# Loads of the first pair in halves on two queues, column maxima by four maxima instead of a reduce, and a head in another order

## The chip, the cores and the metric

The kernel runs on one core of a Trainium2 chip. The metric is the device time of one execution in microseconds. The engines of the core are named as in the profile: PE (matrix products and transposes), DVE (VectorE), ACT (ScalarE), POOL (GpSimd) and SP, which here only issues transfers.

## The reference, cut to what matters

```
q_s = exp(q - max(q, axis=-1));  q_s /= sum(q_s, axis=-1) + 1e-9
k_s = exp(k - max(k, axis=2));   k_s /= sum(k_s, axis=2) + 1e-9     # over the sequence
kv  = einsum('bhsd,bhse->bhde', k_s, v)
att = einsum('bhsd,bhde->bhse', q_s, kv)          # q, k, v: (8, 8, 576, 64)
x   = att.transpose(0, 2, 1, 3).reshape(4608, 512)
out = maximum(x @ w_in, 0)**2 @ w_out             # 512 -> 2048 -> 512
```

The maximum of q is taken along a row of 64; that of k along the sequence, for each head and column.

## The kernel before

A block is one batch entry of 576 rows, handled as four pairs of heads; block 0 and block 1 prepare their attention with the steps named below, later blocks with other code that the change leaves alone. Each tile `kt`, `qt`, `vt` holds one pair as 128 partitions x 2 heads x 5 records x 64: partition p of the lower half holds five neighbouring rows of the sequence (320 rows), one of the upper half four (256 rows), the fifth being a padding. So the column maximum of k is taken in two steps: along the five records of a partition, then across partitions by a transpose.

The steps of block b and pair p carry the two digits behind their names. `Lk`, `Lq`, `Lv` load. `kmax` (DVE) reduces `kt` to `m`, 128x128; `T` (PE) transposes it; `mc` (DVE) takes the maximum of each row; `spread` (PE) puts it back along the columns; `ke` (DVE) subtracts it from k, one operand being the PSUM bank of `spread`; `kexp` (ACT) is the exponential; `kv` (PE) multiplies with v and with ones; `rs`, `rr` (DVE) make the reciprocal sums and `kvn` (ACT or DVE) scales. On the side of q: `qm` (DVE) the row maximum, `qsub` (POOL) subtracts it from `qt` into `qn`, `qexp` (ACT), `qs` (DVE) sums, `qadd` (POOL), `rc` (DVE) the reciprocal `qs`, `qmul` (POOL) `qn<-qn,qs`, then `qt4`, `qt1` (PE) turn it, `cp`, `cps` (ACT) copy it out, `at` (PE) multiplies with kvn, `xhi` (ACT) and `xlo` (DVE) split the result into two parts for the FFN, and `atl`, `left`, `XL` keep the last 64 rows.

A weight chunk of 512 KB goes through `L` (SP; `raw_i` for w_in, `raw_o` for w_out), `low` and `t` (ACT), `s1` and `s2` (DVE: `bank<-bank,raw` and `w<-raw,bank`), `hi` (ACT: `wi<-w` or `wo<-w`) and `lo` (POOL: `wi<-w,wi`). The FFN of block 0 is `h` (PE: products `x_hi,wi` and `x_lo,wi`), `relu` (ACT), `rm` (DVE), `ghi` (ACT), `glo` (POOL) and `o` (PE). `Z` are products of zeros that keep PE running; 28 of them, the beats, stand at the start. `warm` is one small exponential on ACT.

Every engine works through its instructions in the order in which the program names them: the wrapper `InOrder` chains each to the one before on its engine. That order is a table of tokens, `ORDER`, for the start and for blocks 0 and 1 with the FFN of block 0; a second table, `LIST`, gives all the rest. SP issues its transfers in that order too. Since every call passes through the wrapper, nearly all instructions show its line, L290 before and L292 after; they are told apart by their tiles.

In the instruction lists below, kt_78, kt_79, kt_99 and kt_102 are k of the pairs 0 to 3 of block 0; block 1 uses kt_78 and kt_79 in turn.

Of the kernel before, what the change touches and what calls it, by code (L numbers as in the profile page):

```python
# [50 lines left out]
ORDER = """
Lk00 Lq00 Lk00b warm qm00 qsub00 Lq01 qexp00 qm01 kmax00 qs00 Lk01 Li0 kmax01 T01:0 qsub01 qexp01 qadd00 rc00 Lk02
Lq02 qs01 qadd01 Lq03 T00:1 mc00 mc01 Z3:2 spread01 rc01 kmax02 ti0 lowi0 s1i0 Li1 Lv01 ke01 kexp01 Z4:2 T02:2
qmul01 qt101:3 Lk03 qm02 spread00 qt401:4 cps01 mc02 Lv00 qm03 Li2 qmul00 qt400:5 cp00 qt100:6 Z5:0 kv01:0 s2i0 ti1
Lv02 ke00 Lk10 cps00 spread02 qsub03 qexp03 kmax03 lowi1 qsub02 qexp02 Z3:3 T03:3 qs03 rs01 rr01 kexp00 mc03 Lv03
Li3 cp01 Z3:5 kv00:5 Lq10 spread03 kvn01 at01:1 atl01:6 qadd03 rc03 qmul03 qt403:4 lowi2 qs02 qadd02 rs00 rr00 kvn00
ke02 kexp02 rc02 qmul02 hii0 cp03 atl00:0 ke03 kexp03 s1i1 s2i1 ti2 padv00 kmax10 qt103:5 cps03 at00:2 Lo0 hii1 loi1
kv02:3 rs02 rr02 kvn02 xhi00 qt402:4 kv03:5 cp02 at02:3 Li4 T10:4 s1i2 xlo00 xhi01 rs03 rr03 kvn03 h1_0:2 xlo01
xhi02 loi0 mc10 s2i2 at03:1 left00 lowi3 Lo1 qm10 ti3 xlo02 xhi03 lowo0 qt102:5 hii2 Lk11 Lv10 qsub10 s1i3 s2i3 hii3
xlo03 spread10 ke10 loi2 qexp10 Lo2 h0_0:0 h0_1 qs10 cps02 h1_1 h1_2 h1_3 loi3 Li5 h0_2 to0 s1o0 lowo1 h2_0:3 h2_1  # L60
h2_2 relu1 h3_0:1 kexp10 Lk12 qadd10 rc10 qmul10 lowi4 left01 s2o0 to1 rm1 h0_3 ghi1 glo1 h2_3 kmax11 atl03:4 s1o1
s2o1 padv01 Lo3 ti4 s1i4 left03 hio1 atl02:5 qt410:2 kv10:6 cp10 s2i4 loo1 rs10 rr10 T11:4 h3_1 mc11 h3_2 relu0 rm0
kvn10 hii4 lowo2 spread11 ke11 h3_3 to2 at10:2 loi4 h4_0:0 Li12 ghi0 kmax12 qt110:6 hio0 left02 T12:4 mc12 relu3
h4_1 h4_2 h4_3 loo0 kexp11 Lq11 s1o2 spread12 s2o2 late xhi10 xlo10 lowi5 glo0 o0_3:5 o1_3 o0_0:2 o1_0 hio2 ti5 loo2
ke12 o0_2:4 o1_2 relu2 s1i5 Li6 Lo4 s2i5 lowo3 to3 hii5 loi5 qm11 cps10 o0_1:6 o1_1 Lk20 qsub11 rm2 h5_0:3 h5_1 h5_2
h5_3 s1o3 s2o3 XL03 lowi12 lowi6 ghi2 glo2 o2_3 o2_1 o2_2 o2_0 lowo4 rm3 ghi3 glo3 Li7 ti6 XL00 lowi7 hio3 loo3 o3_3
o3_0 o3_1 o3_2 relu4 Lv12 qexp11 kmax20 kexp12 Lq12 XL01 relu5 XL02 s1i6 s2i6 hii6 loi6 h6_0:1 h6_1 h6_2 h6_3 Lk13
rm4 qs11 qadd11 to4 s1o4 s2o4 Lo5 ghi4 hio4 glo4 loo4 o4_3 o4_2 o4_0 o4_1 atl10:0 Li8 qm12 qsub12 ti7 rm5 ghi5
kv12:3 glo5 lowo5 s1i7 s2i7 hii7 loi7 kmax13 relu6 rm6 h7_0:1 to5 s1o5 lowi8 s2o5 qexp12 qs12 qadd12 h7_1 h7_2 h7_3
rc11 qmul11 left10 T13:0 hio5 ti8 s1i8 Lo6 lowo6 rs12 rr12 kvn12 s2i8 to6 s1o6 qt411:3 Li9 loo5 o5_0 Lv11 o5_1 relu7  # L70
rm7 s2o6 hii8 loi8 o5_3 kv11:1 mc13 ghi6 glo6 ti9 cp11 lowi9 Lo7 lowo7 spread13 hio6 loo6 h8_0:3 h8_1 h8_2 Li10 ke20
rs11 rr11 kvn11 s1i9 s2i9 rc12 qmul12 Lo8 lowo8 at11:1 Li13 Lo10 ke13 to7 s1o7 s2o7 hii9 xhi11 lowi10 o6_3 loi9
xlo11 qt111:0 cps11 ti10 s1i10 s2i10 o5_2 ghi7 lowo10 glo7 o6_0 atl11:0 left11 Li15 hio7 loo7 to8 s1o8 s2o8 Lo11
hii10 h8_3 relu8 o6_2 hio8 rm8 h9_0:1 h9_1 h9_2 h9_3 relu9 o6_1 Lk21 o7_3 lowi15 qt412:0 ghi8 Li11 lowi11 kmax21
kexp13 loo8 loi10 o7_0 cp12 ti11 s1i11 s2i11 rm9 qt112:3 cps12 Lo9 o7_1 Lq13 qm13 lowo9 to9 hii11 o7_2 s1o9 glo8
o8_3 Lo13 at12:0 xhi12 h10_0:3 h10_1 h10_2 h10_3 XL11 Lv13 loi11 h11_0:1 h11_1 xlo12 kv13:0 h11_2 ghi9 glo9 Lq20
h11_3 qsub13 lowo11 relu10 Lo14 Li14 s2o9 ti12 hio9 loo9 o9_3 o8_1 o9_1 rm10 atl12:3 qexp13 s1i12 s2i12 to10 s1o10
s2o10 hii12 loi12 relu11 Lo12 Lv20 lowi13 qs13 qadd13 ti13 kexp20 lowi14 Lo15 Lq21 o8_0 o9_0 s1i13 hio10 loo10 rs13
rr13 kvn13 s2i13 rm11 lowo14 Lv21 WA0 WA1 ko0 ko1 to11 o8_2 o9_2 ghi10 ghi11 h12_0:0 h12_1 h12_2 h12_3 rc13 qmul13
s1o11 s2o11 ti14 s1i14 qsub20 Lq22 hio11 lowo12 qt413:1 left12 XL10 glo10 o10_2 o10_3 Lk22 hii13 relu12 qt113:3  # L80
o10_1 lowo13 cps13 atl13:3 left13 XL13 rm12 kv20:0 s2i14 loo11 XL12 loi13 h13_0:3 h13_1 h13_2 h13_3 hii14 qexp20
o10_0 glo11 o11_3 o11_0 o11_2 o11_1 loi14 to12 cp13 h14_0:1 h14_1 h14_2 h14_3 lowo15 ke21 kexp21 s1o12 s2o12 hio12
loo12 ti15 s1i15 s2i15 relu13 rm13 ghi12 glo12 o12_2 o12_3 o12_1 to13 hii15 loi15 s1o13 s2o13 hio13 loo13 qn20 o12_0
h15_0:3 h15_1 h15_2 h15_3 Lv22 WA2 WA3 ko2 ko3 ghi13 relu14 to14 s1o14 s2o14 to15 glo13 o13_3 o13_1 o13_2 hio14
loo14 o13_0 s1o15 s2o15 hio15 rm14 ghi14 glo14 h16_0:1 relu15 rm15 ghi15 glo15 Bw20 Lk23 WA4 ko4 o14_3 qsub21 at13:3
loo15 o15_3 xhi13 xlo13 o14_0 o15_0 B20 rs20 h16_1 rr20 qexp21 ev3 S3 qn21 ev0 S0 ko6 Bw21 h16_2 o14_1 o15_1 ev1
qh20 ql20 kf20 h16_3 relu16 rm16 ghi16 S1 B21 glo16 o14_2 o15_2 ev2 S2 kh20 kl20 Lq23 h17_0:3 h17_1 h17_2 h17_3
""".split()


# [1246 lines left out]
```

## Time and profile before

| | |
|---|---|
| median of three runs (lowest, highest) | 838.47 us (838.05, 840.71) |
| the profiled execution, its own time | 838.89 us |
| its span, first to last instruction | 837.1 us |
| granted clock of PE, mean | 1.000 |
| busy: PE, DVE, ACT, POOL | 99%, 65%, 58%, 34% |
| HBM, over the span | 214 GB/s |

The span is what the trace covers; 1.8 us of the execution lie around it. Busy shares are means over the whole run. The head, some 47 us in which the first products are prepared, is where the engines other than PE are nearly full, and its rows have to be read by themselves.

### The profile page before, as it was taken

The page shows a single profiled execution, that of the slowest core. Times are in us where ns is not written, and L with a number is a line of the kernel's source. Part 1 is how long each engine was busy: PE and PEld are TensorE (multiplying, and loading weights), DVE is VectorE, ACT ScalarE, POOL GpSimd, SP SyncE. Part 2 cuts the span into 40 slices and gives each one's busy share as a digit, 9 for nine tenths or more (in the row PEclk, how much of TensorE's full clock was granted, in tenths as well). Part 3 has the DMA queues.
Part 4 walks back from the last instruction along what each step waited for, and adds up shares of the span by engine and source line. Part 5 has one row for each costly group of instructions (what it writes and reads, how often), then busy time and mean ns, then how long its engine had stood idle before and what let it go on. Part 6 is the DMA issues. An engine that isn't in the chain of part 4 may idle for free.

```text
span 837.1 us, 12969 instructions
## 1 busy us (share of the span) xinstructions
PE 828.8 (99%) x4286; PEld 678.2 (81%) x4286; DVE 540.8 (65%) x1098; ACT 486.7 (58%) x898; POOL 288.2 (34%) x269
## 2 busy tenths in 40 slices
PE   8999999999999999999999999999999999999997
PEld 6778787888888888888888888888888888888886
DVE  7898888878787789957687887653257132222421
ACT  4888866666656656676667455566464144444411
POOL 4578654467667656242322342211004000000000
PEclk9999999999999999999999999999999999999999
...
GB/s 240 270 186 299 279 287 214 327 215 98 211 256 249 227 283 259 277 281 258 234 252 245 283 159 213 271 187 189 172 233 177 98 227 156 163 166 154 186 55 50
DMA packets 156594, 179.65 MB, mean 215 GB/s; under 512 B 51696, under 2 KB 120304, under 8 KB 156528
## 3 DMA queue, kind: packets, MB, share of 16 engines
...
HBM read 133.69 MB, written 45.09 MB: 214 GB/s over the span
## 4 chain that ended last, share of the span: by engine, by line
PE 90%; DVE 4%; DMA 2%; issue 1%; POOL 1%; ACT 1%; SPq 1%; DVEq 0%; POOLq 0%; ACTq 0%
PE bank L290 90%; DVE m L290 1%; DMA raw_o<-in_moe_w_out_dram 1%; DMA qt<-in_q_dram 1%; SPq L290 1%; DMA raw_i<-in_moe_w_in_dram 0%; POOL qs L290 0%; DVE qs L290 0%; DVE g_lo L290 0%; DVE w L290 0%; POOL qn L290 0%; DVE xf L290 0%; DVE bank L290 0%; DVE r L290 0%; DVE qm L290 0%
## 5 line engine op out<-in xcount | busy, mean ns | idle before, releaser
L290 PE MATMUL bank<-wp,g 128*128 128x512 f32 x648 | 160.7, 390 | 0.0
L290 PEld LDWEIGHTS bank<-wp,g 128*128 128x128 f32 x648 | 120.6, 188 | 24.9
L290 PE MATMUL bank<-x_hi,wi 128*128 128x512 f32 x384 | 131.3, 396 | 0.0
L290 PE MATMUL bank<-xh_T,wp 128*128 128x512 f32 x384 | 130.7, 390 | 0.0
L290 PE MATMUL bank<-wo,g_hi 128*128 128x512 f32 x384 | 120.3, 394 | 0.0
L290 PE MATMUL bank<-xh_B,wp 128*128 128x512 f32 x288 | 98.0, 390 | 0.0
L290 POOL TENSOR_TENSOR qs<-qT,qs 64x640 fp32r<-64x640 f32 (+1 forms) x40 | 64.2, 1604 | 94.4 <-ACT qs L290 63.1
L290 DVE TENSOR_TENSOR c<-c,bank 128x512 f32<-128x512 f32 x48 | 32.9, 686 | 86.7 <-ACT c L290 86.4
L290 PEld LDWEIGHTS bank<-xh_T,wp 128*128 128x128 f32 x384 | 72.1, 188 | 16.3 <-ACT bank L290 1.2
L290 PEld LDWEIGHTS bank<-x_hi,wi 128*128 128x128 f32 x384 | 72.2, 188 | 15.9 <-DVE x_lo L290 0.4
L290 ACT ACTIVATE far<-far 128x512 f32<-128x512 f32 x96 | 60.6, 632 | 41.1 <-DVE far L290 39.9
L290 PEld LDWEIGHTS bank<-wo,g_hi 128*128 128x128 f32 x384 | 70.5, 188 | 14.8 <-ACT g_hi L290 0.4
L290 PE MATMUL bank<-wo,g_lo 128*128 128x512 f32 x192 | 75.0, 391 | 0.0
L290 PE MATMUL bank<-x_lo,wi 128*128 128x512 f32 x192 | 74.9, 390 | 0.0
L290 PE MATMUL bank<-xl_T,wp 128*128 128x512 f32 x192 | 74.8, 389 | 0.0
L290 PE MATMUL bank<-wo_back,g 128*128 128x512 f32 x288 | 71.4, 389 | 0.0
L290 DVE TENSOR_TENSOR g<-far,g 128x512 fp32r<-128x512 f32 x48 | 35.7, 781 | 43.5 <-ACT g L290 43.4
L290 DVE TENSOR_TENSOR far<-far,bank 128x512 f32<-128x512 f32 x48 | 32.9, 685 | 47.7 <-PE bank L290 47.5
L290 PEld LDWEIGHTS bank<-xh_B,wp 128*128 128x128 f32 x288 | 54.1, 188 | 11.6
L290 PEld LDWEIGHTS bank<-wo_back,g 128*128 128x128 f32 x288 | 53.6, 188 | 11.0
L290 POOL TENSOR_TENSOR qn<-qn,qs 128x640 f32<-128x640 f32 x30 | 37.8, 1261 | 69.6 <-DVE qs L290 47.0
L290 ACT CAST g<-far 128x512 fp32r<-128x512 f32 x48 | 27.5, 619 | 49.7 <-PE bank L290 49.4
...
## 6 DMA issues: line engine op xcount, KB each, us to landing
...
```

The costliest lines, as they stand in the source:

```text
L290: ins = f(*args, **kwargs)
```

## The change

Three edits, and a new table.

1. q and k of the first pair: the lower half of each (160 KB) is issued by SP, the upper half (128 KB) by ACT, as separate tokens. Before, both halves of that q were issued by ACT, and of that k the lower by SP and the upper by ACT as its third transfer.
2. `kmax` of all pairs of blocks 0 and 1 (`K_MAX_PAIRS`): four tensor_tensor maxima of 128x128, each with two operands in SBUF and the last three working on the result `m` of the one before, instead of one reduce of 128x640.
3. `K_LESS_POOL` is an empty set, and the token `mbc` that goes with it stands nowhere in the table: no instruction comes of them.
4. `ORDER` is another sequence of the same tokens and of the new `Lq00b`; `LIST` is the same.

```
+K_MAX_PAIRS = {0, 1, 2, 3, 4, 5, 6, 7}
+K_LESS_POOL = set()
...
 ORDER = """
-Lk00 Lq00 Lk00b warm qm00 qsub00 Lq01 qexp00 qm01 kmax00 qs00 Lk01 Li0 kmax01 T01:0 qsub01 qexp01 qadd00 rc00 Lk02
+Lq00 Lk00 Lq00b qm00 qsub00 Lk00b Lq01 qexp00 kmax00 Li0 qm01 qs00 Lk01 qsub01 kmax01 warm T01:0 qexp01 qs01 Lq03
...
-        if (b, pr, n) == (0, 0, 0):
-            units["Lk00b"] = lambda: e.act.dma_start(dst[HALF:, :, :HIGH, :], hi)
+        if (b, pr) == (0, 0) and n < 2:
+            units[f"L{'kq'[n]}00b"] = lambda: e.act.dma_start(dst[HALF:, :, :HIGH, :], hi)
             e.sp.dma_start(dst[:HALF], lo)
         elif n < 2 or b == 0:
-            on = e.act if (b, pr, n) == (0, 0, 1) else e.sp
-            on.dma_start(dst[:HALF], lo)
-            on.dma_start(dst[HALF:, :, :HIGH, :], hi)
+            e.sp.dma_start(dst[:HALF], lo)
+            e.sp.dma_start(dst[HALF:, :, :HIGH, :], hi)
...
         def kmax():
             s["m"] = attn_pool.tile([P, 2, D], F32, name="m", tag=f"m{i}")
+            if n in K_MAX_PAIRS:
+                e.dve.tensor_tensor(s["m"], kk[:, :, 0], kk[:, :, 1], op=ALU.max)
+                for j in range(2, LOW):
+                    e.dve.tensor_tensor(s["m"], s["m"], kk[:, :, j], op=ALU.max)
+                return
             e.dve.tensor_reduce(s["m"], kk.rearrange("p h j d -> p h d j"), axis=AX.X, op=ALU.max)
```

How instructions move, at three places.

DVE, at k of pair 2 of block 0 (kt_99), before; `qs` is the reciprocal that POOL's `qn<-qn,qs` waits for, bank_95 holds a weight chunk:

```order
L290 TENSOR_REDUCE mc<-bank_88 128x1
L290 RECIPROCAL qs<-qs 128x10
L290 TENSOR_REDUCE m<-kt_99 128x128
L290 SCALAR_TENSOR_TENSOR bank_95<-bank_95,raw_i_201 128x512
L290 TENSOR_TENSOR ke<-kt_79,bank_88 128x640
```

The same place on DVE after the change:

```order
L292 RECIPROCAL qs<-qs 128x10
L292 TENSOR_TENSOR m<-kt_99 128x128
L292 TENSOR_TENSOR m<-m,kt_99 128x128 x3
L292 TENSOR_TENSOR ke<-kt_79,bank_88 128x640
L292 SCALAR_TENSOR_TENSOR bank_95<-bank_95,raw_i_196 128x512
```

The neighbours stay, and the `ke` of pair 1 stands ahead of the weight step.

DVE, at k of the first pair of block 1 (kt_78), before; x_lo_76 is the FFN's input of block 0:

```order
L290 SCALAR_TENSOR_TENSOR w<-raw_i_235,bank_95 128x512
L290 TENSOR_REDUCE m<-kt_78 128x128
L290 TENSOR_SCALAR rs<-bank_91 128x1
L290 RECIPROCAL rs<-rs 128x1
L290 TENSOR_SCALAR kvn_82<-bank_91,rs 64x64 x2
L290 SCALAR_TENSOR_TENSOR bank_95<-bank_95,raw_i_265 128x512
L290 TENSOR_TENSOR x_lo_76<-bank_90,x_hi_75 128x512
```

The same place on DVE after:

```order
L292 SCALAR_TENSOR_TENSOR w<-raw_i_249,bank_95 128x512
L292 TENSOR_TENSOR m<-kt_78 128x128
L292 TENSOR_TENSOR m<-m,kt_78 128x128 x3
L292 TENSOR_TENSOR x_lo_76<-bank_90,x_hi_75 128x512
L292 TENSOR_SCALAR rs<-bank_91 128x1
L292 RECIPROCAL rs<-rs 128x1
L292 TENSOR_SCALAR kvn_82<-bank_91,rs 64x64 x2
L292 SCALAR_TENSOR_TENSOR bank_95<-bank_95,raw_i_264 128x512
```

The first `x_lo` now follows the maxima at once; the sums and `kvn` of pair 2 and a weight step come behind it. On POOL, the order of the first two `wi` subtractions is exchanged there.

DVE, at k of pair 2 of block 1 (kt_78 again), before; bank_92 holds `spread` of pair 1, and the transpose of `m` writes it next:

```order
L290 TENSOR_SCALAR kvn_82<-bank_94,rs 64x64 x2
L290 TENSOR_TENSOR ke<-kt_79,bank_92 128x640
L290 TENSOR_REDUCE m<-kt_78 128x128
L290 TENSOR_REDUCE mc<-bank_92 128x1
L290 SCALAR_TENSOR_TENSOR bank_95<-bank_95,raw_o_517 128x512
```

The same place on DVE after:

```order
L292 TENSOR_SCALAR kvn_82<-bank_94,rs 64x64 x2
L292 TENSOR_TENSOR m<-kt_78 128x128
L292 TENSOR_TENSOR m<-m,kt_78 128x128 x3
L292 TENSOR_TENSOR ke<-kt_79,bank_92 128x640
L292 SCALAR_TENSOR_TENSOR bank_95<-bank_95,raw_o_490 128x512
L292 TENSOR_REDUCE mc<-bank_92 128x1
```

The maxima have moved ahead of `ke`, and a weight step has come between `ke` and `mc`.

On SP, the first weight chunk now stands ahead of k of pair 1, and the chunk 1 of w_out behind chunk 2 of w_out, k and v of block 1 and chunk 5 of w_in.

## Rows read from the trace of the kernel before

**Rows 1.** Chain of work that ended last, whole span: start us, us, what.
```profile
194.58 637.71 PE bank L290 x3178
```

**Rows 2.** Waits of PE from 46 to 837 us: us in total, times, longest.
```profile
PE bank L290 <- POOL qs L290: 0.3, 1, 0.3
```

**Rows 3.** Stretch 20 to 40: busy by engine, granted clock, DMA share, GB/s.
```profile
20.00:40.00 20.00, 19.43 (x189) 14.47 (x188) 18.01 (x38) 17.82 (x38) 11.71 (x14) 1.00 1.00 267
```

**Rows 4.** Groups by line and form, DVE, whole span: busy us, mean ns.
```profile
L290 DVE TENSOR_REDUCE m<-kt 128x128 f32<-128x640 f32 x32 | 41.8, 1312 | 1.5 <-DMA kt<-in_k_dram 1.4
```

**Rows 5.** Timeline, DVE and POOL around 374 and 325: start us, us, what.
```profile
374.27 0.60 DVE L290 TENSOR_TENSOR kvs<-kf,kvs 64x128 fp32r<-64x128 f32 x2
...
325.08 2.67 DVE L290 TENSOR_TENSOR kvs<-kf,kvs 64x128 fp32r<-64x128 f32 x2
...
324.64 1.67 POOL L290 TENSOR_TENSOR xl_B<-xl_B,xh_B 128x512 fp32r<-128x512 f32 x1 [4.30 <-DVE T L290]
326.27 1.33 POOL L290 TENSOR_TENSOR xl_T<-T,xh_T 128x512 fp32r<-128x512 f32 x1
```

**Rows 6.** Timeline of DVE, a dependent pair of a weight chunk.
```profile
24.23 0.69 DVE L290 SCALAR_TENSOR_TENSOR bank<-bank,raw_i 128x512 uint32<-128x512 uint32 x1
24.95 0.69 DVE L290 SCALAR_TENSOR_TENSOR w<-raw_i,bank 128x512 uint32<-128x512 uint32 x1
```

**Rows 7.** Timeline of DVE and POOL at k of pair 2, block 0.
```profile
12.64 1.28 DVE L290 TENSOR_REDUCE m<-kt 128x128 f32<-128x640 f32 x1
13.84 0.69 DVE L290 SCALAR_TENSOR_TENSOR bank<-bank,raw_i 128x512 uint32<-128x512 uint32 x1
...
12.87 2.48 POOL L290 TENSOR_TENSOR qn<-qn,qs 128x640 f32<-128x640 f32 x2 [0.40 <-DVE qs L290]
```

**Rows 8.** Timeline of DVE, POOL, PE at the first k of block 1.
```profile
25.55 1.30 DVE L290 TENSOR_REDUCE m<-kt 128x128 f32<-128x640 f32 x1
...
28.78 0.69 DVE L290 TENSOR_TENSOR x_lo<-bank,x_hi 128x512 fp32r<-128x512 f32 x1
...
27.30 2.51 POOL L290 TENSOR_TENSOR wi<-w,wi 128x512 fp32r<-128x512 f32 x2 [1.82 <-ACT wi L290]
...
29.53 0.19 PEld L290 LDWEIGHTS bank<-x_hi,wi 128*128 128x128 f32 x1 [0.39 <-DVE x_lo L290]
```

**Rows 9.** Timeline of DVE, POOL, PE at k of pairs 1 and 2, block 1.
```profile
38.32 1.33 DVE L290 TENSOR_REDUCE m<-kt 128x128 f32<-128x640 f32 x1
...
44.69 0.82 DVE L290 TENSOR_TENSOR ke<-kt,bank 128x640 f32<-128x640 f32 x1
45.42 1.31 DVE L290 TENSOR_REDUCE m<-kt 128x128 f32<-128x640 f32 x1
...
39.45 1.28 POOL L290 TENSOR_TENSOR g_lo<-r,g_hi 128x512 fp32r<-128x512 f32 x1 [0.78 <-ACT g_hi L290]
...
43.90 1.29 POOL L290 TENSOR_TENSOR wi<-w,wi 128x512 fp32r<-128x512 f32 x1 [0.21 <-ACT wi L290]
46.05 1.28 POOL L290 TENSOR_TENSOR wo<-w,wo 128x512 fp32r<-128x512 f32 x1 [0.85 <-ACT wo L290]
...
41.85 0.33 PE L290 MATMUL bank<-ident,m 128*128 128x128 f32 x1
...
46.79 0.33 PE L290 MATMUL bank<-ident,m 128*128 128x128 f32 x1
```

**Rows 10.** Chain of work in 0 to 60 us: start us, us, what.
```profile
2.43 4.82 DMA qt<-in_q_dram
...
10.14 1.20 DVE m L290
...
24.92 8.45 DMA raw_o<-in_moe_w_out_dram
...
33.38 3.75 DMA raw_i<-in_moe_w_in_dram
```

**Rows 11.** Timeline of ACT, the second w_out chunk's first step.
```profile
35.88 0.66 ACT L290 ACTIVATE raw_o<-raw_o 128x512 uint32<-128x512 uint8 x1
```

More of the change, by code (lines that the diff above doesn't have):

```diff
@@ L51 @@
 ORDER = """
-Lk00 Lq00 Lk00b warm qm00 qsub00 Lq01 qexp00 qm01 kmax00 qs00 Lk01 Li0 kmax01 T01:0 qsub01 qexp01 qadd00 rc00 Lk02
[L53 to L86, printed above, removed]
@@ L87 @@
-qh20 ql20 kf20 h16_3 relu16 rm16 ghi16 S1 B21 glo16 o14_2 o15_2 ev2 S2 kh20 kl20 Lq23 h17_0:3 h17_1 h17_2 h17_3
+Lq00 Lk00 Lq00b qm00 qsub00 Lk00b Lq01 qexp00 kmax00 Li0 qm01 qs00 Lk01 qsub01 kmax01 warm T01:0 qexp01 qs01 Lq03
+qadd00 rc00 Lk02 Lq02 mc01 T00:1 mc00 spread01 qadd01 rc01 Z3:2 kmax02 ti0 Lv01 ke01 Lk03 lowi0 Li1 s1i0 kexp01 qm03
+Z4:2 T02:2 Lv00 Lv02 Li2 spread00 mc02 qm02 qmul01 qt101:3 cps01 qt401:4 qmul00 Z5:0 s2i0 qt100:6 qsub03 qt400:5 cps00
+Li3 ke00 cp00 kv01:0 Z3:5 spread02 qexp03 kmax03 ti1 Lq10 qs03 qsub02 qexp02 Z3:3 rs01 T03:3 mc03 kexp00 kv00:5
@@ new lines @@
+spread03 rr01 cp01 kvn01 at01:1 qadd03 qs02 Lk10 rc03 atl01:6 Lv03 lowi1 qadd02 rs00 rr00 qmul03 lowi2 qt403:4 kvn00
+rc02 ke02 hii0 kexp02 qmul02 atl00:0 Lo0 ke03 kexp03 cp03 s1i1 s2i1 padv00 kmax10 qt103:5 at00:2 kv02:3 hii1 cps03
+xhi00 xlo00 rs02 rr02 kvn02 qt402:4 ti2 kv03:5 cp02 T10:4 xhi01 Li4 s1i2 rs03 loi0 rr03 at02:3 kvn03 xlo01 xhi02 Lo2
+loi1 h1_0:2 s2i2 left00 lowi3 ti3 mc10 at03:1 qm10 qt102:5 xlo02 xhi03 hii2 Lk11 Lv10 qsub10 Li5 s1i3 s2i3 lowo0
+qexp10 Lo1 h0_0:0 hii3 h0_1 h0_2 cps02 spread10 loi2 xlo03 ke10 qs10 left01 h1_1 to0 h1_2 h1_3 h2_0:3 loi3 h3_0:1
@@ new lines @@
+kexp10 s1o0 qadd10 lowo1 padv01 h2_1 h2_2 rc10 relu1 qmul10 s2o0 rm1 to1 h0_3 ghi1 lowo2 lowi4 s1o1 s2o1 kmax11
+atl03:4 ti4 qt410:2 h2_3 hio1 left03 glo1 Li12 cp10 atl02:5 Lk12 kv10:6 late s1i4 loo1 s2i4 rs10 Lo3 T11:4 h3_1 mc11
+XL03 h3_2 rr10 relu0 rm0 kvn10 hii4 spread11 h3_3 at10:2 to2 hio0 qt110:6 ghi0 relu3 loi4 lowi12 kmax12 ke11 T12:4
+left02 kexp11 h4_0:0 s1o2 loo0 h4_1 mc12 xhi10 h4_2 spread12 Li6 h4_3 Lq11 s2o2 xlo10 lowi5 glo0 o0_0:2 o0_3:5 ti5
+hio2 Lo4 loo2 o1_0 cps10 lowo3 s1i5 ke12 relu2 o0_1:6 o0_2:4 o1_2 s2i5 hii5 to3 loi5 o1_3 Lk20 rm2 rm3 qm11 qsub11
@@ new lines @@
+o1_1 h5_0:3 h5_1 h5_2 h5_3 s1o3 lowi6 s2o3 ghi2 glo2 o2_2 o2_3 ghi3 glo3 hio3 relu4 loo3 o3_3 ti6 qexp11 kexp12 o2_0
+Li7 XL00 Lk13 kmax20 lowi7 o3_0 lowo4 Lo5 s1i6 qs11 s2i6 to4 qadd11 Lv12 Li8 relu5 o2_1 o3_1 o3_2 rm4 hii6 Lq12 loi6
+s1o4 s2o4 hio4 loo4 XL01 XL02 ghi4 h6_0:1 h6_1 h6_2 h6_3 qm12 qsub12 glo4 o4_1 o4_0 o4_2 o4_3 atl10:0 lowo5 rm5 ti7
+s1i7 ghi5 s2i7 to5 s1o5 glo5 qexp12 hii7 loi7 kv12:3 Lv11 kmax13 s2o5 rc11 relu6 lowi8 Lo6 qmul11 rm6 ti8 qs12 left10
+hio5 qadd12 s1i8 s2i8 T13:0 ghi6 h7_0:1 mc13 h7_1 Lo10 lowo6 h7_2 rs12 rr12 to6 h7_3 kvn12 loo5 o5_3 o5_0 o5_1 s1o6
@@ new lines @@
+s2o6 relu7 hii8 qt411:3 Lq13 qm13 Li9 glo6 rm7 kv11:1 ti9 lowi9 cp11 spread13 loi8 h8_0:3 h8_1 hio6 loo6 ke20 h8_2
+rs11 s1i9 rr11 Lo8 lowo8 Lo7 lowo7 kvn11 s2i9 ke13 rc12 qmul12 to7 at11:1 s1o7 Li13 o5_2 o6_0 hii9 loi9 xhi11 s2o7
+xlo11 Li10 lowi10 o6_3 ti10 s1i10 qt111:0 ghi7 glo7 Li15 s2i10 cps11 hio7 loo7 h9_0:1 atl11:0 to8 lowo10 left11 h9_1
+s1o8 s2o8 Lo11 hii10 h8_3 relu8 rm8 hio8 o6_1 Li11 lowi11 o7_1 Lo9 o6_2 ti11 kexp13 h9_2 ghi8 h9_3 relu9 o7_0 loi10
+Lk21 o7_3 qt412:0 kmax21 lowo9 loo8 lowi15 glo8 o8_3 o7_2 s1i11 rm9 s2i11 cp12 qt112:3 cps12 to9 Lo14 hii11 Lq20
@@ new lines @@
+at12:0 h10_0:3 h10_1 Lv13 h10_2 h10_3 loi11 ghi9 XL11 lowo11 h11_0:1 h11_1 s1o9 Li14 s2o9 h11_2 qsub13 kexp20 h11_3
+Lo13 xhi12 xlo12 relu10 glo9 hio9 loo9 o8_1 o9_3 o9_1 rm10 atl12:3 ti12 s1i12 s2i12 to10 s1o10 kv13:0 Lk22 qexp13
+s2o10 Lo12 relu11 lowi13 hii12 loi12 Lv20 qs13 ti13 hio10 loo10 lowi14 rs13 rr13 o8_0 rm11 ko0 o9_0 Lv21 kvn13 s1i13
+WA0 s2i13 lowo14 o8_2 o9_2 ghi10 Lo15 h12_0:0 ghi11 h12_1 ko1 h12_2 h12_3 qadd13 rc13 qmul13 to11 s1o11 lowo12 s2o11
+qsub20 Lq22 hio11 qt413:1 XL10 hii13 glo10 left12 o10_3 relu12 o10_2 qt113:3 ti14 o10_1 cps13 Lq21 lowo13 atl13:3
@@ new lines @@
+left13 rm12 kv20:0 loi13 h13_0:3 h13_1 h13_2 s1i14 XL13 XL12 glo11 s2i14 to12 loo11 o11_2 o11_1 h13_3 cp13 hii14 loi14
+qexp20 o10_0 o11_3 s1o12 h14_0:1 h14_1 ke21 s2o12 h14_2 hio12 ko2 ko3 WA1 ti15 s1i15 lowo15 s2i15 h14_3 ghi12 loo12
+o11_0 relu13 rm13 to13 s1o13 hii15 loi15 glo12 o12_3 o12_2 qn20 ghi13 o12_0 Lv22 s2o13 to14 s1o14 s2o14 glo13 relu14
+h15_0:3 h15_1 h15_2 h15_3 o12_1 Lk23 rm14 hio13 loo13 o13_3 o13_2 to15 h16_0:1 o13_1 kexp21 hio14 o13_0 WA2 WA3 loo14
+ghi14 relu15 s1o15 s2o15 hio15 WA4 glo14 Bw20 rm15 ghi15 rs20 glo15 qsub21 at13:3 loo15 ko4 o14_0 o15_0 o14_3 o15_3
@@ L88 @@
+xhi13 o14_1 xlo13 B20 ev3 h16_1 ko6 Lq23 S3 rr20 h16_2 qexp21 qn21 ev0 Bw21 S0 h16_3 o15_1 qh20 ql20 relu16 kf20 rm16
+ghi16 glo16 ev1 kh20 o14_2 kl20 o15_2 h17_0:3 h17_1 h17_2 h17_3 ev2 S1 S2 B21
 """.split()
@@ L492, in ke, with mbc @@
             s["ke"] = attn_pool.tile([P, 2, LOW, D], F32, name="ke", tag="q_hi" if i else "ke")
+            if n in K_LESS_POOL:
+                mb = s["ms"].rearrange("p (h o d) -> p h o d", h=2, o=1)
+                e.pool.tensor_tensor(s["ke"], kk, mb.broadcast_to([P, 2, LOW, D]), op=ALU.subtract)
+                return
             mb = s["mb"].rearrange("p (h o d) -> p h o d", h=2, o=1)
             e.dve.tensor_tensor(s["ke"], kk, mb.broadcast_to([P, 2, LOW, D]), op=ALU.subtract)
+        def mbc():
+            s["ms"] = w_pool.tile([P, P], F32, name="ms", tag="raw", bufs=RAWB)
+            e.act.copy(s["ms"], s["mb"])
         def kexp():
@@ L592, in pair_units @@
         for f in (
-            kmax, T, mc, spread, ke, kexp, qm, qsub, qexp, qs, qadd, rc, qmul, kv, padv, rs, rr, kvn_,
+            kmax, T, mc, spread, mbc, ke, kexp, qm, qsub, qexp, qs, qadd, rc, qmul, kv, padv, rs, rr, kvn_,
             qt4, cp, qt1, cps, at, xhi, xlo, atl, left, XL,
```

## The prediction

> **What bounds the kernel now.** I read three views first. The chain of work that ended last is TensorE (PE) without a break for its last 637.71 us [rows 1], and the waits of PE say that from 46 us to the end it waits 0.3 us in all [rows 2]. So from 46.8 us on PE has always something to do, and a microsecond that the head loses before that point can't be won back: it comes out at the end. The same holds for a microsecond won. The change is worth what it does to the time at which PE gets its work in the first 47 us, and what new waits it makes while blocks 0 and 1 are prepared. There the page of stretches shows VectorE (DVE) busy 18.01 us of 20 from 20 to 40 us and the DMA engines full (share 1.00 at 267 GB/s) [rows 3]. DVE is the engine to watch: it feeds PE there, and it has no slack.
>
> **The maxima by themselves: nothing.** One reduce over five records has a mean of 1312 ns [rows 4], and the next instruction starts 1.20 us after its start (12.64 to 13.84) [rows 7]. Its replacement is four maxima of 128 columns, both operands in SBUF. The nearest row is `kvs<-kf,kvs`, 128 columns from SBUF twice on half the partitions: two in 0.60 us, 0.30 each, at a time when GpSimd (POOL) is idle [rows 5]. Each of the last three needs the one before; a dependent pair, `bank` and `w`, starts 0.72 us apart for a duration of 0.69 [rows 6], so 0.03 a link. 4 x 0.30 + 3 x 0.03 = 1.29 us, against 1.20 to 1.31: between -0.02 and +0.1 each. I take 0. There is no gain of time in the edit itself, unless a maximum is shorter than its nearest row.
>
> One figure of a page speaks for the change. The Trainium skill, "VectorE: DVE Perf Modes", section "The TRN2 errata", has a table by which 128 columns from SBUF take 58 + 128 cycles at 0.96 GHz, 194 ns. By that four are 0.78 us and each reduce replaced saves about 0.4. The same section says that the table is too low for single instructions and that (N+151)/0.96 fits fp32 tensor_tensor, which is 291 ns for 128; the 0.30 us of rows 5 agree with the second.
>
> **The maxima beside POOL: this is the cost.** Rows 5 also show the same pair of instructions while POOL works. At 325.08 it takes 2.67 us for 0.60, and POOL has one subtraction of two SBUF tiles under way (324.64, 1.67 us) and another right behind (326.27, 1.33 us). The pair ends when the second POOL operation has ended: each of the two waited for one POOL operation, and POOL's next got in between. That is (2.67 - 0.60) / 2 = 1.03 us for each POOL operation met; the bound above is the whole operation, 1.33. A reduce doesn't suffer: the one at 12.64 takes 1.28 us although POOL's two multiplications of 1.24 start at 12.87 [rows 7]. So the edit turns an instruction that POOL can't disturb into four that POOL can, each of which may let a POOL operation go first.
>
> The Trainium skill, "SBUF — State Buffer", section "Who interferes with whom", states this as a rule: a DVE instruction with two SBUF inputs contends with POOL's reads, and a reduce never does on this chip. It gives no price; the sum below uses rows 5.
>
> Now place by place, with the order after the change.
> - k of pair 2 (`kt_99`), unchanged neighbours. On DVE the four maxima follow the reciprocal `qs`, which also releases POOL's two `qn<-qn,qs`, back to back. Before, the reduce stood there at 12.64 and POOL started at 12.87 [rows 7]. The first maximum gets through, the second and third each let a POOL operation pass: 2 x 1.03 = 2.1, at most 2 x 1.25 = 2.5. I take **+2.3**. Behind it in DVE's queue stand `ke` of pair 1 and all that leads to its kv product, so the delay travels.
> - k of the first pair of block 1 (`kt_78`). Before, the reduce ran at 25.55; POOL's two `wi` subtractions came at 27.30, after waiting 1.82 us for ACT [rows 8]. The table now issues the other of the two first, which needs an ACT cast made early, so it is there when the maxima start, and its twin follows. Two operations met: **+2.1** (1.0 if one, 2.6 at most). Right behind stands `x_lo` of pair 0. It used to start at 28.78, with rs, its reciprocal, two `kvn` products and a 0.70 us weight step between: 28.78 - 26.80 - 0.70 = 1.28 us for the first four. Now: the maxima end at 26.80 + 2.3 + 2.1 = 31.2, `x_lo` adds 0.6, the four 1.28, then PE needs its product with kvn (some 0.4; a transpose of 128 columns takes 0.33 [rows 9]) before the first FFN matmul: 33.5 instead of 29.53 [rows 8]. **+3.9** for PE at this point, both places included. Without any stall the same sum gives 29.1, 0.4 sooner.
> - k of pair 1 of block 1. Before: 38.32 to 39.65, its transpose on PE at 41.85, so 2.2 us of slack [rows 9]. Now two weight steps `s1`, `s2` stand ahead (1.3, as in [rows 6]), which leaves 0.9; POOL has `g_lo` (39.45 before) and a `wo` subtraction around. Two met: 2.06 - 0.9 = **+1.2** (0 to 1.8).
> - k of pair 2 of block 1. Before, `ke` (44.69) and then the reduce (45.42), and the transpose at 46.79 begins as the reduce ends [rows 9]: PE has no slack here. Now the maxima stand ahead of `ke`, and the transpose writes the bank that `ke` reads, so it waits for both. The work is the same, the maxima meet POOL's run of `wo`, `wi`, `wo` (43.90 and 46.05 are two of them), whose inputs from DVE are all made earlier: three, **+3.1** (1.0 to 4.0).
> - The other four: pairs 0 and 1 of block 0 run while POOL has nothing to do at that moment, 0; pair 3 of block 0 meets the end of one `qn<-qt,qm`, and pair 3 of block 1 runs later, when PE has a stock of work: together **+0.5** (0 to 1.7).
>
> **The loads.** q of pair 0 no longer comes in two transfers of one queue, so its maximum `qm` may start up to 0.8 us sooner. But the first transposes need k of pair 1, and this now stands behind the first weight chunk of 512 KB (0.52 MB / 267 GB/s = 2.0 us [rows 3]). q of pair 1, the transfer ahead of it, landed at 2.43 + 4.82 = 7.25 [rows 10]; k of pair 1 is 0.29 MB, 1.1 us more, so 8.4 before and 10.4 now. DVE's reduce of it stands in the chain at 10.14 [rows 10]. **+0.3** (-0.5 to +0.6). Further on, `raw_o` of chunk 1, which landed at 24.92 + 8.45 = 33.37, is now issued behind another `raw_o`, k and v and the `raw_i` that landed at 33.38 + 3.75 = 37.13 [rows 10]. The bytes are the same, so it is the last of them and lands at about 37.1. ACT's step on it ran at 35.88 [rows 11], and a relu stands right behind in ACT's queue: +1.25 if nothing else is late. With PE and DVE 3.9 us later it is covered: 0 in the sum.
>
> The table moves many more tokens. No row prices that; I take 0 and give it 1.5 us either way.
>
> **Sum.** 0.3 + 3.9 + 1.2 + 3.1 + 0.5 = 9.0 us. The profiled execution took 838.89 us (span 837.1 and 1.8 around it), 0.4 above the median of 838.47; 838.89 + 9.0 = 847.9, and on the median 847.5. The bounds: with 1.3 us an operation, 4.7 + 1.75 + 3.9 + 1.7 + 0.6 + 1.5 = 14.2, 852.6; if kt_99 and each of the others meets a single operation, 0.3 + 2.0 + 0.2 + 1.0 = 3.5, 842.
>
> **Rivals.**
> - *No collision.* POOL's subtractions come at other moments, or a maximum of a full tile doesn't take part in what the kvs rows show. Then the head gains 0.4, loses 0.3 to k of pair 1 and 1.25 to the late `raw_o`: +1.1, 839.6, no measurable change. For it: the POOL rows at 27.30 and 46.05 show POOL waiting for ACT before them. Against it: at 12.87 POOL starts 0.23 us behind the very instruction that is replaced, and that neighbourhood stays.
> - *Not slower: the maxima are short.* The 0.30 us of rows 5 is half of a pair; if four in a row overlap more than the two do and take 0.9 us together, DVE gains 0.3 (1.20 - 0.9) at each of the places where it is full; two of them, kt_99 and kt_78, lie on PE's path. With q landing sooner and no collision: -0.4 - 0.6 - 0.5 = -1.5, plus the 1.25 of the `raw_o` if that is not covered: 837.0 to 838.2. It decides from 0.9 us for the four, with POOL clear of them. Against it: each of the four needs the one before, and a dependent pair does not overlap at all [rows 6]. (The table of the Trainium skill's section named above would give this rival; rows 5 speak against it.)
> - *Faster by more.* PE's waits in the head would have to shrink by 2.5 us. The first transposes can't come before k of pair 1, so I see no place for it except a better order later that no row shows.
> - *Absorbed.* Only the collision at kt_99 happens in full and half of it lands in DVE's 2 us of idle between 20 and 40: +1 to +2.5, 839.5 to 841.
>
> **How the numbers follow.** About 0.3%, 2.5 us, is what a measurement of this kernel can tell from no change. Collisions as forecast or some of them, over +2.5: 0.79. No collision 0.08, absorbed 0.04, short maxima 0.04 of which a part goes over the bound, an unseen gain of order 0.05. So slower 0.79, same 0.14, faster 0.07. The range takes the forecast's own 842 to 852.6 and reaches down to the absorbed case and into that without collision: 840 to 853, with some 0.15 outside.
>
> **What would show it.** Right: single maxima `m` of over 1 us on DVE beside POOL's TENSOR_TENSOR, at kt_99 and at kt_78 above all; the sum of the 32 maxima clearly over 32 x 0.30 = 9.6 us; PE's first `x_hi,wi` at about 33.5; new waits of PE for DVE `m` or `ke` between 40 and 55 us; after that PE without waits as before. Wrong: maxima of 0.2 to 0.3 us throughout, the first `x_hi,wi` at 29 or sooner, or PE waits after 60 us, which would mean that the rest of the table costs or brings more than I give it. If ACT waits long for a `raw_o` around 37 us, the loads and not the port were the cost.

## The result and the profile after

| | before | after |
|---|---|---|
| median of six runs (lowest, highest) | 838.35 us (838.03, 841.22) | 851.01 us (848.13, 852.42) |
| ratio of the times, 95% interval | 1 | 1.0129 [1.0112, 1.0147] |
| the profiled execution, its span | 838.89, 837.1 us | 848.59, 846.8 us |
| mean granted clock of PE | 1.000 (profiled) | 0.997 (profiled), 0.991 to 0.998 in the six |

The change makes the kernel slower: by 1.3%, which is 10.8 us, by the ratio, and by 12.7 us on the medians; the two differ because the executions of one kernel spread over 3 to 4 us. The forecast was 847.5 within 840 to 853. The sign and the collisions with POOL came out as written and the sum is 3.5 us below the median, but it charged nearly the whole loss to the maxima, and the experiments show that this is not so.

The page's busy line: PE works 1.4 us longer than before (828.8), DVE 7 us (540.8); the rest of the 9.7 us of longer span is PE waiting.

```profile
PE 830.2 (98%) x4286; PEld 679.4 (80%) x4286; DVE 547.8 (65%) x1122; ACT 486.8 (57%) x898; POOL 287.6 (34%) x269
```

The waits of PE, after: in 0 to 46, in 46 to 60, in 60 to 120 and from 120 us on (what PE waited for, us in total, times, longest). They answer to [rows 2], where 0.3 us stood from 46 us to the end:

```profile
PE bank L292 <- DVE m L292: 1.9, 2, 1.5
...
PE bank L292 <- DVE kvn L292: 1.1, 1, 1.1
...
PE bank L292 <- DVE ke L292: 3.2, 1, 3.2
...
PE bank L292 <- ACT left L292: 1.4, 1, 1.4
PE bank L292 <- POOL g_lo L292: 1.1, 1, 1.1
...
PE bank L292 <- POOL wo L292: 0.7, 1, 0.7
```

Three things are new: longer waits for DVE in the head (3.5 us, 0.5 of it for `mc`, against 0.8 before), 3.2 us for `ke` at 49 us, and 3.2 us more that came after 60 us, where I had seen nothing.

At k of pair 2 of block 0 (the timeline of DVE and POOL, start and duration in us; before, [rows 7]) the maxima take 12.89 to 16.04, 3.15 us from start to the next start, where the reduce took 1.20. POOL's two multiplications pass in between:

```profile
12.89 0.23 DVE L292 TENSOR_TENSOR m<-kt 128x128 f32<-128x128 f32 x1
13.15 2.97 DVE L292 TENSOR_TENSOR m<-m,kt 128x128 f32<-128x128 f32 x3
16.04 0.81 DVE L292 TENSOR_TENSOR ke<-kt,bank 128x640 f32<-128x640 f32 x1
...
13.12 2.53 POOL L292 TENSOR_TENSOR qn<-qn,qs 128x640 f32<-128x640 f32 x2 [0.41 <-DVE m L292]
```

At the first k of block 1 (before, [rows 8]) there are two causes in one row: the maxima meet POOL, but the first of them has also waited 0.59 us for the transfer of `kt`, which it did not before. PE's first FFN product comes at 32.68 (29.53 before; I said 33.5):

```profile
27.71 0.77 DVE L292 TENSOR_TENSOR m<-kt 128x128 f32<-128x128 f32 x1 [0.59 <-DMA kt<-in_k_dram]
28.51 2.07 DVE L292 TENSOR_TENSOR m<-m,kt 128x128 f32<-128x128 f32 x3
30.50 0.69 DVE L292 TENSOR_TENSOR x_lo<-bank,x_hi 128x512 fp32r<-128x512 f32 x1
...
28.83 1.28 POOL L292 TENSOR_TENSOR wi<-w,wi 128x512 fp32r<-128x512 f32 x1 [0.50 <-ACT wi L292]
...
32.68 0.80 PE L292 MATMUL bank<-x_hi,wi 128*128 128x512 f32 x1
```

At k of pair 2 of block 1 (before, [rows 9]) the maxima meet the tail of one POOL operation and two whole ones and take 3.69 us from start to the next start; then `ke` follows, and PE's transpose has waited 3.24 us for both:

```profile
47.71 0.77 DVE L292 TENSOR_TENSOR m<-kt 128x128 f32<-128x128 f32 x1
48.52 2.85 DVE L292 TENSOR_TENSOR m<-m,kt 128x128 f32<-128x128 f32 x3
51.40 0.82 DVE L292 TENSOR_TENSOR ke<-kt,bank 128x640 f32<-128x640 f32 x1
...
47.05 1.28 POOL L292 TENSOR_TENSOR wi<-w,wi 128x512 fp32r<-128x512 f32 x1 [0.96 <-ACT wi L292]
48.29 1.33 POOL L292 TENSOR_TENSOR wo<-w,wo 128x512 fp32r<-128x512 f32 x1
49.58 1.31 POOL L292 TENSOR_TENSOR g_lo<-r,g_hi 128x512 fp32r<-128x512 f32 x1
...
52.27 0.33 PE L292 MATMUL bank<-ident,m 128*128 128x128 f32 x1 [3.24 <-DVE ke L292]
```

The wait for `left` behind 60 us comes from maxima, too. At k of pair 3 of block 1 they meet the tail of a `g_lo` and a `wi` and take 2.62 us to the next start (74.21 to 76.83). A weight step `w` stands behind them on DVE, ACT waits 1.75 us for it, and ACT's `left` is next in ACT's queue. In the kernel that has the same table and reduces (the first experiment), ACT waits 0.38 us at this point and PE not at all:

```profile
74.21 0.68 DVE L292 TENSOR_TENSOR m<-kt 128x128 f32<-128x128 f32 x1
74.92 1.99 DVE L292 TENSOR_TENSOR m<-m,kt 128x128 f32<-128x128 f32 x3
...
74.81 1.29 POOL L292 TENSOR_TENSOR wi<-w,wi 128x512 fp32r<-128x512 f32 x1
...
77.54 0.64 ACT L292 ACTIVATE bank<-raw_i 128x512 f32<-128x512 f32 x1 [1.75 <-DVE w L292]
...
78.37 0.33 PE L292 MATMUL bank<-ident,m 128*128 128x128 f32 x1 [1.37 <-ACT left L292]
```

### The profile page after: what moved, and what is told of

Its sections match the earlier page's. It is cut to its first block, busy times and chain, and to the rows that moved or that the text cites. A ratio compares the mean times of both kernels' runs of the same rounds, so it can differ in the third digit from the quotient of the medians.

```text
span 846.8 us, 12992 instructions
## 1 busy us (share of the span) xinstructions
PE 830.2 (98%) x4286; PEld 679.4 (80%) x4286; DVE 547.8 (65%) x1122; ACT 486.8 (57%) x898; POOL 287.6 (34%) x269
## 4 chain that ended last, share of the span: by engine, by line
PE 87%; DVE 6%; DMA 3%; ACT 1%; SPq 1%; POOL 1%; issue 1%; DVEq 0%; POOLq 0%
PE bank L292 87%; DVE m L292 2%; DMA vt<-in_v_dram 1%; DMA kt<-in_k_dram 1%; SPq L292 1%; DVE w L292 1%; DVE bank L292 1%; ACT bank L292 1%; DVE ke L292 0%; POOL wo L292 0%; POOL qn L292 0%; DVE qs L292 0%; DVE qm L292 0%; ACT r L292 0%; DVE r L292 0%
```

## The experiments

Times are medians; the ratio is to runs of the kernel before on the same chip (838.7 to 839.1 us there). Three chips were used, so two experiments are best compared by their ratios.

**Which part of the change costs it.** Three kernels, each with one part alone.

The changed kernel without the maxima:

```
-K_MAX_PAIRS = {0, 1, 2, 3, 4, 5, 6, 7}
+K_MAX_PAIRS = set()
```

> The changed kernel with its loads and its order, but with one reduce for the column maxima of all eight pairs, as before the change. Port theory (the four maxima wait for POOL's operations): nearly all of the loss goes, 837.5 to 841 us, PE's first x_hi,wi at 29 to 29.8 us, and the wait of 3.2 us of PE for ke at 49 us is under 0.7. Order theory (the table and the loads cost the time): 847 to 851 us, and that wait stays.

Measured: 845.34 us, 1.0077 [1.0062, 1.0092]. Neither theory: the order and the loads cost 6.6 us by themselves, which I had put at 0 within 1.5. PE's first `x_hi,wi` comes at 31.68 (29.53 before), with no maxima anywhere, and ahead of it DVE waits 3.91 us for k:

```profile
28.33 1.25 DVE L292 TENSOR_REDUCE m<-kt 128x128 f32<-128x640 f32 x1 [3.91 <-DMA kt<-in_k_dram]
```

The new table asks for that k behind weight chunk 3 and q of the pair; before, it stood ahead of both. The wait for `ke` is down to 0.86 us; the port theory said under 0.7. With three other waits of PE behind the first product it makes 4.0 us:

```profile
PE bank L292 <- DVE ke L292: 0.9, 1, 0.9
PE bank L292 <- ACT left L292: 0.7, 1, 0.7
...
PE bank L292 <- POOL g_lo L292: 1.6, 1, 1.6
PE bank L292 <- POOL wo L292: 0.8, 1, 0.8
```

With the 2.15 us at the first product these make 6.1 of the 6.3 us by which this span is longer (843.4 against 837.1).

The kernel before with the maxima in all eight places:

```
         def kmax():
             s["m"] = attn_pool.tile([P, 2, D], F32, name="m", tag=f"m{i}")
-            e.dve.tensor_reduce(s["m"], kk.rearrange("p h j d -> p h d j"), axis=AX.X, op=ALU.max)
+            e.dve.tensor_tensor(s["m"], kk[:, :, 0], kk[:, :, 1], op=ALU.max)
+            for j in range(2, LOW):
+                e.dve.tensor_tensor(s["m"], s["m"], kk[:, :, j], op=ALU.max)
```

> The kernel before, with its loads and its order, and only the column maxima of the eight pairs by four maxima. Port theory: slower by 4 to 10 us (842 to 848), the maxima of kt_99 beside POOL's two qn multiplications end about 2 us later than the reduce did. Order theory: within 1 us of before, since the maxima alone take what the reduce takes.

Measured: 848.48 us, 1.0118 [1.0102, 1.0133]: 9.8 us for the maxima alone, just above the upper end of what I gave. 9.8 and 6.6 make 16.4, and the whole change costs 12.7: the two losses partly lie on each other.

The kernel before with the new first loads:

```
-Lk00 Lq00 Lk00b warm
+Lq00 Lk00 Lq00b Lk00b warm
```

and the new branch of `load`.

> The kernel before with only the new first loads: lower halves of q and k of the first pair by SP, q first, upper halves by ACT; the rest of the table as before, so k of pair 1 stays ahead of the first weight chunk. My theory: the first qm starts 1.5 to 2 us sooner, but the first transposes wait for k of pair 1 and for DVE, so PE's first x_hi,wi moves by at most 0.5 us and the time by -0.5 to +0.3 (838 to 838.7). Rival (the head is bound by its first load): 1.5 us faster, 836.5 to 837.

Measured: 838.80 us, 1.0003 [0.9990, 1.0016]. No change that can be measured, although the first `qm` starts at 4.32 instead of 6.18: it is not what the head waits for.

**Is it POOL?** Two kernels with the same instructions, that of before with maxima at kt_99 alone; in the second one token stands earlier, so that POOL's multiplications start after the maxima.

```
         def kmax():
             s["m"] = attn_pool.tile([P, 2, D], F32, name="m", tag=f"m{i}")
+            if n == 2:
+                e.dve.tensor_tensor(s["m"], kk[:, :, 0], kk[:, :, 1], op=ALU.max)
+                for j in range(2, LOW):
+                    e.dve.tensor_tensor(s["m"], s["m"], kk[:, :, j], op=ALU.max)
+                return
```

> The kernel before with four maxima at one place only, pair 2 of block 0 (kt_99), beside POOL's two multiplications. Port theory: the maxima end 2 to 2.5 us later than the reduce, and as DVE is full there the first x_hi,wi on PE and the time move by 1.5 to 2.5 us: 840 to 841. Rival (absorbed by the idle time of DVE between 20 and 26 us): under 0.7 us, 838.5 to 839.2.

```
-... Z3:2 spread01 rc01 kmax02 ti0
+... Z3:2 spread01 kmax02 rc01 ti0
```

> The same one place of maxima (kt_99) in the kernel before, with the same instructions, but the maxima stand ahead of the reciprocal that lets POOL's two multiplications start, so POOL is idle while they run. Port theory: they take 1.2 us as the reduce did, and the time is 838.4 to 839.3, against 840.1 with POOL beside them. Rival (four dependent instructions, or the later multiplications, cost it): 840 or more again.

Measured: 840.13 us, 1.0021 [1.0008, 1.0034], and 838.91 us, 1.0004 [0.9992, 1.0015]. The two intervals overlap, so the rows have to decide. The timelines of DVE and POOL, first with POOL beside them:

```profile
12.31 0.27 DVE L290 TENSOR_TENSOR m<-kt 128x128 f32<-128x128 f32 x1
12.62 2.92 DVE L290 TENSOR_TENSOR m<-m,kt 128x128 f32<-128x128 f32 x3
15.46 0.69 DVE L290 SCALAR_TENSOR_TENSOR bank<-bank,raw_i 128x512 uint32<-128x512 uint32 x1
...
12.54 2.52 POOL L290 TENSOR_TENSOR qn<-qn,qs 128x640 f32<-128x640 f32 x2 [0.40 <-DVE qs L290]
```

then with POOL after them:

```profile
12.34 0.27 DVE L290 TENSOR_TENSOR m<-kt 128x128 f32<-128x128 f32 x1
12.64 0.94 DVE L290 TENSOR_TENSOR m<-m,kt 128x128 f32<-128x128 f32 x3
13.50 0.21 DVE L290 RECIPROCAL qs<-qs 128x10 f32<-128x10 f32 x1
...
13.86 2.48 POOL L290 TENSOR_TENSOR qn<-qn,qs 128x640 f32<-128x640 f32 x2 [1.52 <-DVE qs L290]
```

3.15 us against 1.16 for the same four instructions: 1.0 us for each POOL operation that gets between. Alone, they are as fast as the reduce (1.20) and no faster. The Trainium skill, "SBUF — State Buffer", section "Who interferes with whom", says that a DVE instruction with two SBUF inputs contends with a POOL instruction that reads SBUF; these rows agree and add the price.

**Only some places.**

```
+K_MAX_PAIRS = {0, 1, 3, 5}
```

> The changed kernel with four maxima only at pairs 0, 1 and 3 of block 0 and pair 1 of block 1, where its trace shows them with POOL idle or nearly so; the reduce at pair 2 of block 0 and at pairs 0, 2 and 3 of block 1. Port theory: within 0.7 us of the same kernel with reduces everywhere. Rival (four dependent instructions cost by themselves, wherever they stand): half of the loss stays, 843 to 846.

Measured: 846.20 us, 1.0090 [1.0066, 1.0114], 0.9 above the one with reduces everywhere, with intervals that overlap: no cost that can be told from none, and not half of the loss. The two of its four executions with a mean granted clock of 0.997 and 0.999 took 845.26 and 844.36, the two with 0.993 and 0.994 took 847.15 and 848.55.

```
+K_MAX_PAIRS = {0, 1, 2, 3, 4, 5, 7}
```

> The changed kernel with a reduce at pair 2 of block 1 alone; maxima at the other seven. Port theory: PE's wait for ke at 48 us falls from 3.2 to about 0.9 us, and so 2.4 us go. If PE's clock, which falls in some executions after that wait, is part of the loss, the median falls by more than 2.4: from 851.0 to 847 to 848, with mean clocks of 0.996 and more. Rival (the wait turns up again further on): 850 and more.

Measured: 847.86 us, 1.0103 [1.0083, 1.0124]; the wait for `ke` falls from 3.24 to 0.55. On the medians this one place is worth 3.1 us of the 12.7, by the ratios 2.2, and their intervals overlap. The clocks were not what I expected: 0.993 to 0.996. In the profile the granted clock falls in the stretches 12 to 18 and 32 to 38 us, and not behind that wait.

**Where the order's loss comes from.** The changed kernel with reduces, then with maxima, its first 40 transfers on SP in the sequence of before and all else by the new table (of the table, the loads alone move):

```
-... Lq01 qexp00 kmax00 Li0 qm01 qs00 Lk01 ... Li2 Li3 Lq10 Lk10 Lv03 Lo0 Li4 Lo2 ...
+... Lq01 qexp00 kmax00 Lk01 qm01 qs00 Li0 ... Lk10 Lv03 Li3 Lq10 Lo0 Li4 Lo1 ...
```

> The changed kernel with one reduce for all column maxima, and with its first 40 transfers on SP in the sequence of the kernel before (the compute engines keep the new table). Transfer theory (the new table costs time because k of the first pair of block 1, chunk 1 of w_out and q of pair 2 of block 1 are asked for later): 838 to 840 us, no wait of DVE for kt before the maxima of that k, PE's first x_hi,wi below 30 us. Rival (the sequence on DVE, ACT and PE costs it): 843 us and more, as with the new transfers.

> The changed kernel whole, with four maxima everywhere, and only its first 40 transfers on SP in the sequence of the kernel before. If the late transfers hide part of the maxima's waits for POOL, this one shows them by themselves: 846 to 849 us, so 8 to 10 above the same kernel with reduces. If maxima and transfers add up instead, 843 to 845.

Measured: 843.15 us, 1.0049 [1.0028, 1.0070], and 849.56 us, 1.0120 [1.0100, 1.0140]. The sequence of transfers gives back some 2 us where there are no maxima, with intervals that just overlap, and not the 6 that the transfer theory wanted. DVE takes the k of block 1 without a wait, but the first `x_hi,wi` is at 30.59, not below 30. What is left, 4.4 us, can be the order of the engines' own work, the transfers behind the first 40, or a misfit of old transfers and new order: DVE now waits 1.01 and 1.44 us for k of pairs 2 and 3 of block 0. With maxima the sequence gives back 1.4 or nothing (1.0129 [1.0112, 1.0147] for the change itself); the maxima then cost 6.4, not the 8 to 10 that I gave.

Reduces, and k of that pair ahead of weight chunk 3:

```
-... cps00 Li3 ke00 cp00 ... at01:1 qadd03 qs02 Lk10 rc03
+... cps00 ke00 Lk10 Li3 cp00 ... at01:1 qadd03 qs02 rc03
```

> The changed kernel with reduces, and one transfer moved: k of the first pair of block 1 is issued ahead of weight chunk 3 and q of that pair, as in the kernel before. Transfer theory: PE's first x_hi,wi comes 2 us sooner than with the new transfers (29.7 against 31.7), the time falls by 1 to 2.5 us to 843 to 844.5, and the rest of the order's loss (w_out chunk 1, q of pair 2) stays. Rival: the loss comes back further on, 845.

Measured: 845.49 us, 1.0075 [1.0055, 1.0096]: nothing. DVE takes that k at 26.85 without a wait, but now the `x_lo` right behind it waits for ACT's `x_hi`, and the first `x_hi,wi` is at 31.28, 1.75 us later than before the change:

```profile
29.10 0.69 DVE L292 TENSOR_TENSOR x_lo<-bank,x_hi 128x512 fp32r<-128x512 f32 x1 [0.94 <-ACT x_hi L292]
```

At 43 us PE waits 1.34 us for `r`, whose ACT step stands behind a late weight chunk. The rival was right: what one transfer gains, other waits take.

Two kernels begin with the table of before and go on with the new one (reduces, old loads), the first from the first FFN product on:

```
-(table of before, from h1_0:2)
+(the new table's order of all tokens that are left)
```

> The kernel before (its loads, reduces) up to its first FFN product, and from there the new table's order of all tokens that are left. If the order's 6.6 us are made in the head (late k, late v), this is 838.7 to 840.5; if they are made behind it, 843 to 845. My reading of the traces (waits of PE for POOL and ACT between 60 and 135 us add up to 2.4 to 3.2 us, and 0.9 for ke at 48): 842 to 843.5.

the second from the transpose of k of pair 2 of block 1 on:

```
-(table of before, behind T12:4)
+(the new table's order of all tokens that are left)
```

> The kernel before up to the transpose of k of pair 2 of block 1 (46.8 us in its trace), with its loads and reduces, and the new table's order of what is left. If the waits between 60 and 135 us belong to the late part of the new table: 841 to 842.5, with PE waits for g_lo, left or wo there. If they only follow from a late start: 838.7 to 839.5.

Measured: 845.16 us, 1.0062 [1.0044, 1.0080], and 843.64 us, 1.0045 [1.0032, 1.0058]. Both are above what I gave. The part behind 50 us alone costs 4.6 of the 6.6 us on the medians, 3.8 by the ratio. Giving back the old head gains nothing that can be told, but this does not show that the new head is free. The first product is in time again (29.49), and in place of the 2.15 us stands a wait that neither whole table has: ACT waits for chunk 1 of w_out and PE then waits for `r` (ACT and PE):

```profile
40.90 0.67 ACT L290 ACTIVATE raw_o<-raw_o 128x512 uint32<-128x512 uint8 x1 [4.35 <-DMA raw_o<-in_moe_w_out_dram]
...
42.91 0.63 PE L290 MATMUL bank<-ident,qn 128*128 128x128 f32 x4 [3.22 <-DVE r L290]
```

In the second, DVE waits for q of pair 2 of block 1, which the new table asks for behind k of pair 3 and two weight chunks. POOL's `qsub` needs the `qm` of it, and the new table sets that `qsub` ahead of a `g_lo` that it stood behind before. That `g_lo` has its `g_hi` by 63.8 and runs at 66.55; PE waits for it (DVE, ACT, POOL and PE):

```profile
64.43 0.82 DVE L290 TENSOR_REDUCE qm<-qt 128x10 f32<-128x640 f32 x1 [1.83 <-DMA qt<-in_q_dram]
...
63.21 0.61 ACT L290 CAST g_hi<-r 128x512 fp32r<-128x512 f32 x1
...
65.33 1.26 POOL L290 TENSOR_TENSOR qn<-qt,qm 128x640 f32<-128x640 f32 x1 [0.54 <-DVE qm L290]
66.55 2.53 POOL L290 TENSOR_TENSOR g_lo<-r,g_hi 128x512 fp32r<-128x512 f32 x2
...
67.88 0.50 PE L290 MATMUL bank<-wo,g_lo 128*128 128x512 f32 x1 [1.27 <-POOL g_lo L290]
```

The same chain stands in the profile after, where `qm` waits 2.24 us for q and PE 1.14 us for `g_lo`, and so does a wait for `wo`.

## Why the prediction was right, and where not

- *PE has no slack after 46 us:* right. In the profile after, 3.15 us at the first FFN product, 3.24 us for `ke` and 3.2 us behind 60 us make 9.6 of the 9.7 us of longer span.
- *Maxima by themselves, 0:* right, 1.16 us alone against 1.20. The 194 ns that one table of the Trainium skill's "VectorE: DVE Perf Modes" ("The TRN2 errata") gives for a maximum is not met; the rows of single maxima clear of POOL show 0.23 to 0.29 us.
- *1.03 us for each POOL operation:* right, 1.0.
- *kt_99, +2.3:* 2.0 on DVE, 1.5 at PE's first FFN product, 1.4 in the time. In that profile the maxima start 0.33 us sooner than the reduce did (12.31 against 12.64), so the next step is 1.62 late, and nearly all of that travels, as I had said.
- *The first k of block 1, +3.9 at PE's first product with both collisions:* measured +3.15, but on another way, so that the number is partly luck. I followed the weights' transfers past each other and not that of this very k, which the table sets behind a weight chunk and a q. Without any maxima DVE waits 3.91 us for it, and PE is 2.15 us late there (31.68). In the change the delays ahead of it used up most of that wait, which is why it reads 0.59, and behind it comes a mix of one whole operation and a tail, not two. Nor is this k the whole of it: where it comes in time, `x_lo`, which the new table puts directly behind it, waits for ACT's `x_hi`, and PE is still 1.75 us late.
- *Pair 1 of block 1, +1.2:* 0.1. The transpose is at 45.12, 3.27 late, where the first product was 3.15 late; only a tail of `g_lo` was met.
- *Pair 2 of block 1, +3.1:* right in the wait, 3.24 us, of which 0.86 stand there without maxima as well. With a reduce there 2.7 us of wait go, and 2.2 to 3.1 us of time.
- *The other four, +0.5:* too low. Pair 3 of block 1 alone costs PE 1.37 us, through `left`; the stock of work that I had given PE at that point did not cover it.
- *k of pair 1 behind the first weight chunk, +0.3:* right. It came at 10.38 (10.4 forecast), the transposes at 11.80 instead of 11.49.
- *The late w_out chunk, 0 because covered:* right in the change, and its uncovered price, 1.25, was too low for one of the two kernels that show it: 3.2 us of PE in the kernel with the old head, 1.3 in the one with the early k.
- *All other tokens, 0 within 1.5:* wrong, and this is the step that failed. The order alone costs 6.6 us. I had looked for no rows that price the moves behind 50 us; PE waits after 60 us, which I had named as a sign of this, are there. In the profile after, the waits for `g_lo` and `wo` make 1.8 us of them; the 1.4 us for `left` belong to the maxima.

So the sum came near by luck, through two errors that cancel: the maxima were charged 8.7 us and add only 5.7 to the new order (851.01 against 845.34; 4.4 by the ratios), while the order was charged nothing. On the old order the same maxima cost 9.8, so how the loss is shared depends on which part is taken out first. The rival without collisions (839.6) would have been wrong by 6 us even where no collision happens.

One loss was in no case of mine: the clock. In the profiled execution of the kernel with maxima and old transfers PE waits 3.23 us for `ke`, and then the granted clock is 0.50, the 1.2 GHz level, for 6 us and more, in which PE is busy for 5 (stretches of 2 us: busy PE, PEld, DVE, ACT, POOL, then PEclk, DMA share, GB/s):

```profile
48.00:50.00 2.00, 0.00 (x0) 0.00 (x0) 1.93 (x3) 0.44 (x2) 1.61 (x2) 0.87 0.01 4
50.00:52.00 2.00, 1.01 (x3) 0.91 (x4) 1.97 (x5) 1.03 (x2) 0.00 (x0) 0.50 0.00 0
52.00:54.00 2.00, 2.00 (x6) 1.52 (x6) 1.68 (x3) 2.00 (x6) 0.10 (x1) 0.50 0.04 8
54.00:56.00 2.00, 2.00 (x8) 1.61 (x7) 0.24 (x2) 0.98 (x2) 1.19 (x1) 0.50 0.00 0
56.00:58.00 2.00, 2.00 (x10) 1.63 (x9) 2.00 (x4) 0.72 (x2) 0.02 (x1) 0.92 0.00 0
```

By an estimate, half of PE's busy time at 0.50 is lost, 0.5 + 1 + 1 = 2.5 us on top of the wait. The profiled execution of the change had the same wait and no fall behind it. Its one fall lies in the head, beside PE's waits for DVE, with 0.77 and 0.88 in the neighbouring stretches:

```profile
14.00:16.00 2.00, 2.00 (x6) 1.16 (x4) 1.93 (x3) 0.00 (x0) 1.65 (x2) 0.50 0.98 295
```

A shorter wait can be followed by a fall, too. In the kernel with maxima at some places only, PE waits 1.87 us for `g_lo`, and then come:

```profile
72.00:74.00 2.00, 2.00 (x6) 1.56 (x7) 2.00 (x3) 2.00 (x4) 1.92 (x2) 0.55 1.04 307
74.00:76.00 2.00, 2.00 (x8) 1.57 (x6) 2.00 (x5) 0.77 (x2) 1.70 (x3) 0.59 1.07 377
```

The same kernel with reduces everywhere has a wait of 1.86 us ahead of 29.45 and keeps 1.00. The profiled execution of the change is among the fastest of its six, 848.59; the three with mean clocks of 0.991 to 0.994 took 850.9 to 851.4. That the clock makes this difference fits, but the clock's course in those runs was not recorded, and one run at 0.996 took 852.42.

Still open: which moves of the new table, of transfers or of the engines' own work, cost what. The chains above, that of `left` included, are read from rows; none was undone by itself.
